# Idle matmuls of the opening read a framework constant instead of a tile that the kernel clears itself

One core of one Trainium2 chip. The metric is the device time of one execution in microseconds, lower is better; the span is the stretch from the first to the last instruction of a profiled execution, some 1.7 us shorter.

## The reference

```python
def reference(q, k, v, n_global, n_local, w_in, w_out, s, b):
    # attention: batch 4, 8 heads, 768 positions, head size 64; a key is kept if it is
    # one of the first 8 positions or one of the 96 positions up to the query
    scores = q @ k.T / sqrt(64) - slope[head] * dist        # others: -1e9
    x = softmax(scores) @ v                                 # heads joined: 3072 x 512
    # feed-forward
    r = maximum(x @ w_in, 0)                                # 512 -> 2048
    return (s * r * r + b) @ w_out                          # 2048 -> 512
```

The outputs are float32; the kernel computes in bf16 with float32 sums.

## The kernel before

The change touches nothing but the first microseconds. The parts that matter, with cuts marked:

```python
    # first loads: k on the queue of SyncE, q on that of ScalarE, in two halves each
    for h2 in range(2):
        for n, eng in enumerate((nc.sync, nc.scalar)):
            f = work.tile([P, H // 2, GB * D], F32, name="first", tag="first", bufs=4)
            eng.dma_start(f[:], pairs_of(srcs[n], 0, h2 * H // 2, H // 2))
            first_f32[h2, n] = f
    nc.scalar.preload_act_table_set("natural_log_exp_and_others")
    # ...
    idle = gpool.tile([P, 4 * P], BF16, name="idle", tag="gsum1", bufs=1)
    nc.vector.memset(idle[:], 0.0)
    for vb in vbuf:
        nc.vector.memset(vb[:, :, :, D:VW], 1.0)
    # ...
    def warm(n, w=2 * P):       # matmuls whose result nobody reads
        ps = ps_h.tile([P, w], F32, name="ps_w", tag="psh")
        for _ in range(n):
            nc.tensor.matmul(ps[:], lhsT=idle[:, 0:P], rhs=idle[:, 0:w], start=True, stop=True)
    # ...
    warm(9, 4 * P)
    cast_first(0, 0, cp)        # first half of k to bf16, VectorE
    cast_first(0, 1, acp)       # first half of q, ScalarE
    # ...
    qk_first(0, 0, cp)          # transposes on TensorE, copied out by VectorE
    qk_first(0, 1, acp)         # the same for q, copied out by ScalarE
    open_bias((0, 1))           # four 128x384 bias matmuls
    cast_first(1, 0, cp)        # second halves
    cast_first(1, 1, acp)
    for part in range(2):       # scores of the first two units
        for i in (0, 1):
            u[i][1](part)
    run(u[0][2])                # exponential of the first unit, ScalarE
    warm(4)
    qk_first(1, 0, cp)          # second halves: transposes and copies
    qk_first(1, 1, acp)
    # ... attention and feed-forward follow, TensorE densely busy
```

The softmax here doesn't subtract the row's maximum and nothing guards it: scores larger than these inputs give would overflow.

## Time and profile before

| | before |
|---|---|
| time, median of the first three executions | 208.71 us (208.68 to 208.73) |
| span of the profiled execution | 207.1 us |
| first idle matmul | 1.20 us into the span |
| first matmul that does work (transposes) | 5.30 us |
| second group of scores, the step at which the opening is done | 9.55 us |

The opening counts because it delays all the rest.

The chain lists what each moment stood on, so an instruction that is not in it delays nothing by its own duration. And TensorE's rate is read from the steps between equal instructions in sequence. The trace itself also keeps a record of the granted clock; its first entry (full) is at 7.15 us, and that is what the steps say too.

### The profile page before, as it was taken

Reading aid. Unit: us, or ns where it says so; the run is one execution under the profiler, and the core shown is the slowest. Engines: PE = TensorE matmul, PEld = TensorE weight load, DVE = VectorE, ACT = ScalarE, POOL = GpSimd, SP = SyncE. Lnnn points to the kernel's source line nnn. Section 1 sums busy time; section 2 is a strip of 40 time slices with the busy share of each in tenths; the row PEclk is TensorE's granted clock in tenths of the full one; section 3 lists DMA queues with packets and bytes.
Section 4 is the critical chain, followed back from the end, with each engine's and each line's share of the span. In section 5 each row is a group of like instructions: output and inputs, shape, how many; then the busy total and the mean of one; then the engine's idle time right before and its main releaser. Section 6 shows DMA issues by size and latency. Waiting matters only on the chain.

```text
span 207.1 us, 5315 instructions
## 1 busy us (share of the span) xinstructions
PE 201.7 (97%) x2183; PEld 160.3 (77%) x2191; DVE 160.7 (78%) x338; ACT 128.4 (62%) x198; POOL 69.7 (34%) x90
## 2 busy tenths in 40 slices
PE   7999999999999999999999999999999999999993
PEld 2678885557876685878888898888888889888883
DVE  7686689977988956799799974699866696737974
ACT  5776669585975648686664595663695764476200
POOL 8985233999455402805502808200000000000000
PEclk9999999999999999999999999999999999999999
DMA  6999999999999999999999999996360300240006
GB/s 162 173 179 200 207 206 177 156 152 136 124 149 134 156 141 224 121 250 209 136 214 181 106 141 179 167 212 69 53 205 3 93 10 3 57 149 0 0 8 197
DMA packets 110836, 28.17 MB, mean 136 GB/s; under 512 B 97852, under 2 KB 109308, under 8 KB 110812
## 3 DMA queue, kind: packets, MB, share of 16 engines
q0 software_dynamic: 76000, 13.11, 86.8%
q1 hardware_dynamic: 33612, 14.13, 37.7%
q10 hardware_dynamic: 1200, 0.59, 1.1%
q8 instruction: 17, 0.28, 0.6%
q14 instruction: 7, 0.06, 0.1%
HBM read 27.26 MB, written 6.29 MB: 162 GB/s over the span
## 4 chain that ended last, share of the span: by engine, by line
PE 95%; DMA 2%; DVE 1%; issue 0%; ACT 0%
PE ps L619 41%; PE ps L819 24%; PE ps L667 13%; PE ps_s L441 6%; PE ps_av L495 5%; DMA first<-in_k_dram 2%; PE ps_t L351 1%; PE ps_s L517 1%; PE ps_t L327 1%; PE ps_x L591 1%; PE ps_s L416 1%; PE ps_s L532 1%; PE ps_av L558 1%; PE ps_t L341 0%; PE ps_last L819 0%
## 5 line engine op out<-in xcount | busy, mean ns | idle before, releaser
L619 PE MATMUL ps<-xT,w_in_bf 128*128 128x256 bf16 x768 | 90.3, 273 | 0.1
L629 ACT ACTIVATE gT<-ps 128x512 bf16<-128x512 f32 x96 | 55.7, 598 | 46.8 <-PE ps L619 46.6
L619 PEld LDWEIGHTS <-w_in_bf 128*128 128x128 bf16 x768 | 73.0, 98 | 9.4 <-DVE xT L594 0.2
L450 ACT ACTIVATE pt<-ps_s 128x1024 bf16<-128x1024 f32 (+1 forms) x44 | 39.3, 946 | 3.0 <-PE ps_s L441 3.0
L667 PE MATMUL ps<-w_out_bf,gT 128*128 128x512 bf16 x120 | 28.7, 380 | 0.5 <-issue 0.2
L457 DVE TENSOR_TENSOR pt<-pt,tmpl 128x1024 bf16<-128x1024 bf16 (+1 forms) x40 | 24.5, 645 | 3.6 <-ACT pt L450 3.5
L819 PEld LDWEIGHTS <-gsum 128*128 128x128 bf16 x256 | 24.1, 98 | 3.8 <-DVE gsum L782 0.5
L108 POOL DMA_DIRECT2D vb<-in_v_dram x24 | 21.4, 907 | 4.3 <-DMA w_out_bf<-in_moe_w_out_dram 3.0
L793 DVE TENSOR_TENSOR gT<-gT 128x1024 bf16<-128x1024 bf16 x20 | 13.7, 687 | 11.7 <-ACT gT L629 11.7
L667 PEld LDWEIGHTS <-gT 128*128 128x128 bf16 x128 | 11.7, 98 | 13.0
L466 DVE TENSOR_TENSOR xn<-ps_av,rc 128x256 bf16<-128x256 f32 x48 | 20.4, 425 | 1.7
L819 PEld LDWEIGHTS <-gT 128*128 128x128 bf16 x200 | 18.6, 98 | 2.3
L465 DVE RECIPROCAL rc<-ps_av 128x4 f32<-128x4 f32 x48 | 8.6, 179 | 12.4 <-PE ps_av L495 10.7
L495 PEld LDWEIGHTS <-pt 128*128 128x128 bf16 x320 | 14.4, 97 | 2.7 <-DVE xn L466 0.7
L632 DVE TENSOR_TENSOR gT<-gT 128x512 bf16<-128x512 bf16 x32 | 12.9, 421 | 3.6 <-ACT gT L629 3.3
L495 PE MATMUL ps_av<-vb,pt 128*128 128x65 bf16 x208 | 15.4, 193 | 0.0
L819 PE MATMUL ps<-w_out_bf,gsum 128*128 128x256 bf16 x128 | 15.3, 273 | 0.0
L819 PE MATMUL ps<-wsub,gsum 128*128 128x256 bf16 x128 | 15.1, 273 | 0.0
L116 POOL DMA_DIRECT2D nat<-in_q_dram x14 | 12.5, 890 | 6.8 <-DMA nat<-in_q_dram 2.8
L116 POOL DMA_DIRECT2D nat<-in_k_dram x14 | 12.4, 884 | 5.8 <-DMA w_in_bf<-in_moe_w_in_dram 2.4
L122 POOL COPY gate<-xT 1x1 bf16<-1x1 bf16 x6 | 1.5, 258 | 37.3 <-DMA xT<-xn 37.3
L819 PE MATMUL ps<-w_out_bf,gT 128*128 128x256 bf16 x120 | 13.9, 273 | 0.0
(112 smaller groups left out, 232.8 us busy)
## 6 DMA issues: line engine op xcount, KB each, us to landing
out_dram<-o_q SPq DMA_DIRECT2D x15, 256.0 KB, 2.5
vb<-in_v_dram POOLq DMA_DIRECT2D x24, 128.0 KB, 7.5
nat<-in_k_dram POOLq DMA_DIRECT2D x22, 128.0 KB, 6.9
nat<-in_q_dram POOLq DMA_DIRECT2D x22, 128.0 KB, 6.9
w_out_bf<-in_moe_w_out_dram POOLq DMA_DIRECT2D x4, 512.0 KB, 16.3
w_in_bf<-in_moe_w_in_dram POOLq DMA_DIRECT2D x4, 256.0 KB, 7.5
w_in_bf<-in_moe_w_in_dram POOLq DMA_DIRECT2D x2, 512.0 KB, 11.5
out_dram<-o_sb SPq DMA_DIRECT2D x4, 256.0 KB, 6.0
```

Source lines behind the costliest of these rows:

```text
L108: nc.gpsimd.dma_start(vbuf[b % 2][:, sb, :, 0:D], rows_of(v, b, sb))
L116: nc.gpsimd.dma_start(t[:, n, i, :, :], rows_of(srcs[n], b, sb))
L450: nc.scalar.activation(pt[:, :, 0:ncol], ps[:, :, 0:ncol], ACT.Exp, scale=QSCALE)
L457: nc.vector.tensor_tensor(pv, pv, m.rearrange("p h a c -> p h (a c)"), ALU.mult)
L466: nc.vector.tensor_tensor(dst, av[:, :, :, 0:D], rc[:].to_broadcast((P, 2, 2, D)), ALU.mult)
L495: nc.tensor.matmul(av[:, i, hi, 0 : D + 1], lhsT=pt[:, hi, c * P : (c + 1) * P], rhs=vv, start=(n == 0), stop=(n == len(terms) - 1),)
L619: nc.tensor.matmul(ps[:, i, :], lhsT=w_in_bf[:, kc, fc * P : (fc + 1) * P], rhs=xT[j][:, kc, :], start=(kc == 0), stop=(kc == KC - 1),)
L629: nc.scalar.activation(gs, ps[:], ACT.Relu)
L632: nc.vector.tensor_tensor(gs, gs, gs, ALU.mult)
L667: nc.tensor.matmul(po[:], lhsT=g_of(j)[:, fc, tb * P : (tb + 1) * P], rhs=w_out_bf[:, fc, :], start=(fc == 0), stop=(fc == FC - 1),)
L793: outs.append(lambda: nc.vector.tensor_tensor(gs, gs, gs, ALU.mult))
L819: nc.tensor.matmul(ps[:, tb, cs], lhsT=stat[:, fc, tb * P : (tb + 1) * P], rhs=mov[:, fc, cs], start=(fc == 0), stop=(fc == NH - 1),)
```

## The change

The idle matmuls run before there is any input, so that TensorE's clock is full when the work comes. (Full clock means here the moment from which equal matmuls follow each other at half the earlier distance: in the trace before, 128x384 matmuls 0.32 us apart at 6.45, and 0.16 us at 8.74; 128x128 transposes 0.107 us apart at 5.49, and 0.056 us at 8.33.) The intent is to start them sooner: they read a constant that the framework writes before it lets the engines go (on GpSimd, at 0.31 us; the first transfers are issued at 0.74), so that no memset on VectorE stands in front of them; the time won is filled by a tenth matmul.

```diff
-    idle = gpool.tile([P, 4 * P], BF16, name="idle", tag="gsum1", bufs=1)
-    nc.vector.memset(idle[:], 0.0)
 # ...
-            nc.tensor.matmul(ps[:], lhsT=idle[:, 0:P], rhs=idle[:, 0:w], start=True, stop=True)
+            nc.tensor.matmul(
+                ps[:],
+                lhsT=nc.const_aps.tensor(1.0, (P, P), BF16),
+                rhs=nc.const_aps.tensor(1.0, (P, w), BF16),
+                start=True,
+                stop=True,
+            )
 # ...
-    warm(9, 4 * P)
+    warm(10, 4 * P)
```

## The prediction

> **What bounds the kernel now.** I started with the first part of the page, the busy shares, to see which engine is the bound over the whole span.
>
> ```profile
> span 207.1 us, 5315 instructions
> PE 201.7 (97%) x2183; PEld 160.3 (77%) x2191; DVE 160.7 (78%) x338; ACT 128.4 (62%) x198; POOL 69.7 (34%) x90
> ```
>
> TensorE's matmuls fill 97% of the span. The chain that ended last says the same: "PE 95%; DMA 2%; DVE 1%". So time is to be had only where TensorE waits or runs slowly, and the change touches only the first 9 us. I therefore asked for the chain of work in that stretch (start, duration, what), because it shows what each microsecond of the opening stands on.
>
> ```profile
> 0.74 3.73 DMA first<-in_k_dram
> 4.46 0.02 issue
> 4.49 0.77 DVE nat L260
> 5.25 0.05 issue
> 5.30 1.04 PE ps_t L327 x8
> 6.34 1.11 PE ps_s L416 x4
> 7.45 0.44 PE ps_s L441 x12
> 7.89 0.54 PE ps_w L161 x4
> 8.44 0.46 PE ps_t L327 x8
> 8.92 0.59 ACT qx L331
> ```
>
> The nine idle matmuls at the start, the ones the change is about, are not in it. The first 4.46 us belong to a load from HBM that is issued at 0.74, then a cast on VectorE; only at 5.30 does TensorE join the path. The four later idle matmuls (0.54 us at 7.89) are in it. The third view is the timeline of the opening (start, duration, engine, line, instruction, count, idle before and its releaser).
>
> ```profile
> 0.86 0.27 DVE L151 MEMSET idle<- 128x256 uint32 x1 [0.86 <-PEq L1235]
> 1.20 4.02 PE L161 MATMUL ps_w<-idle 128*128 128x512 bf16 x9 [1.20 <-DVE idle L151]
> 1.60 0.15 PEld L161 LDWEIGHTS <-idle 128*128 128x128 bf16 x1 [0.28 <-issue]
> 2.02 0.15 PEld L161 LDWEIGHTS <-idle 128*128 128x128 bf16 x1 [0.28 <-issue]
> 4.49 0.76 DVE L260 CAST nat<-first 128x512 bf16<-128x512 f32 x1 [0.36 <-DMA first<-in_k_dram]
> 6.45 0.15 PEld L416 LDWEIGHTS <-open_bf 128*128 128x128 bf16 x1 [0.17 <-issue]
> 6.77 0.15 PEld L416 LDWEIGHTS <-open_bf 128*128 128x128 bf16 x1 [0.17 <-issue]
> ```
>
> The idle matmuls wait until 1.20 for the memset. Two weight loads in sequence lie 0.43 us apart, which is the step from one 128x512 matmul to the next. The 128x384 bias matmuls still step by 0.32 us at 6.45 and 6.77. Later the same form steps by half of that: the pair at 8.74 takes 0.48 us in all and the pair at 10.29 0.49 us, against 1.32 us for the four at 6.13. So TensorE runs at half rate up to about 7.1 us and at full rate from the next matmuls (7.38) on, although the page's row of granted clock shows 9 tenths from the first slice; I trust the steps. The idle matmuls exist to bring that moment forward.
>
> [...]
>
> **The change, part by part.** I compared the instruction order of the two builds on each engine. With line numbers set aside, it differs in three places: one memset fewer at the head of VectorE; no wait in front of TensorE's first weight load; ten instead of nine idle pairs. The later four keep their place. The constant is written by the framework on GpSimd, ahead of the barrier that starts all engines.
>
> Memset: 1 x 0.27 us leaves VectorE. Its followers move up, but the chain on VectorE that ends with a memset at 3.96 to 4.13 then waits for the load that lands at 4.46 (0.36 us of idle before the cast). So this saves nothing on the path: 0.
>
> First start: TensorE no longer waits for the memset. The SyncE and ScalarE queues issue their first transfers at 0.74, the earliest an engine is past the barrier here; TensorE passes it about as late as VectorE or a little earlier (0.86 at most). I take 0.80. The head start is 1.20 - 0.80 = 0.40 us.
>
> Tenth matmul: ten cold ones hold the array for 10 x 0.427 = 4.27 us, from 0.80 to 5.07; nine held it from 1.20 to 1.20 + 9 x 0.427 = 5.04. The transposes can't start before 5.30, when the cast is done. So the tenth fits before them, 0.2 us to spare, and costs 0; it would begin to cost only if the start slipped beyond 5.30 - 4.27 = 1.03.
>
> What is left is the moment of full clock. Every 1.0 us that it comes earlier while TensorE is on the path (5.30 to about 7.4, the transposes and bias matmuls) saves 0.5 us of half-rate work. If the moment follows the first idle matmul, it moves from 7.1 to 6.7: about one bias matmul more runs at 160 instead of 320 ns, and 0.4 x 0.5 = 0.20 us is saved. ScalarE's copy of q (6.37 + 0.59 = 6.96), which the score matmuls also need, allows this: they now start at 7.38 and would start at 7.18. [...]all of the opening is warm: 8 transposes 0.42 us less, 4 bias matmuls 4 x 0.16 = 0.64 us less; but the copies of k and q, behind the casts, hold the scores to about 6.7 (a gain of 0.68), and the second load of q, cast on ScalarE from 6.92 on, together with the first exponential behind it leave about 0.5 us further on.
>
> Is such a gain passed on to the end? No wait for a load shows up on TensorE between 9 and 36 us, and there TensorE is soon dense: 104 matmuls of L619 in 11.42 us from 20.45 on, 0.110 us each. The loads before that have some room: by the trace's landings, the second block of q is in at 11.99 and first used at about 12.6, v at 10.41 for 10.98, the fourth part of w_in at 19.54 for 20.36. So up to about 0.5 us goes through whole.
>
> Sum: 0 (memset) + 0 (tenth matmul) + a clock term between 0 and 0.5, for which I take 0.22 us.
>
> **The rivals.** [...] Third, reading one element with a step of zero could be slow for TensorE[...]. Nine to ten cold matmuls hide that, but the four of 256 columns at 7.83 are on the path, now 0.11 us apart; at half rate they would cost 4 x 0.11 = 0.44 us more: 209.1. [...]
>
> **Range and chances.** I weigh no move of the moment at 35%, a move with the start (0.2 us) at 40%, the jump (0.5 us) at 15%, a loss by the constant's reading at 10%. The mean is 0.40 x 0.20 + 0.15 x 0.5 - 0.10 x 0.44 = 0.11 us, the likeliest single case 0.20; the 0.22 above leans a little to that case and the jump, and gives 208.71 - 0.22 = 208.49. For noise between sessions I add 0.15 us on either side: 208.05 to 208.85. Faster by 2% would need 4.2 us, more than all of the half-rate work on the path; slower by 2% would need a clock that is lost. Both get 1%.
>
> **What would show it.** The first 128x512 idle matmul should start at about 0.8 and not at 1.20, with steps of 0.427 us; the cast at 4.49 and the transposes at 5.30 should stand still within 0.05 us. If they moved, my claim that the memset and the tenth matmul are free is wrong. The steps of the 128x384 bias matmuls tell the clock: all 0.32 us, no move; one more at 0.16, the move; all 0.16, the jump. The score matmuls of L441 should start at about 7.2 and everything after lie earlier by the same amount, up to the end. The four later idle matmuls should stay 0.11 us apart; 0.21 would be the loss by reading a constant. I would be wrong altogether if the transposes waited for the tenth idle matmul, or if the time moved without any of these steps moving.

Passages are cut from this text, with the cuts marked, because they rested on what no run here shows: a rule for the two rates (the rates themselves are measured, 0.32 and 0.16 us from one bias matmul to the next), the reason for the jump, the first, the second and the fourth rival, and part of the third. The forecast's sum: 0 (memset) + 0 (tenth matmul) + 0.22 us (clock) = 0.22 us, and 208.71 - 0.22 = 208.49. The jump is the case in which the clock is full before the transposes start, so that all of the opening runs at full rate ("warm" in the text; "cold" is half rate). Its 0.5 us is an estimate from the steps and durations of the trace before. That such a case can come, the 15% for it and the 35% for no move were my guess. The 0.427 us is the step of the idle matmuls in that trace, (4.583 - 1.596) / 7.

## More of the kernel before

The prediction shows the lines, up to the copy of q that ends at 9.51; the chain goes on with the second group of scores:

```profile
9.55 0.34 PE ps_s L441 x6
```

## The result, and the profile after

The changed kernel took 208.41 us in the median of six executions (208.33 to 209.05), before 208.69 us in six of the same rounds. The ratio is 0.9992, with a 95% interval from 0.9978 to 1.0006: the same. Ratios here are those of the record, which compares the fast runs of the same rounds, so not quite the ratio of the medians. The span of the profiled execution went from 207.1 to 206.6 us.

The timeline of the kernel after, matmuls and first cast of the opening (start, duration, engine, line, instruction, count, idle before and its releaser):

```profile
0.78 4.42 PE L159 MATMUL ps_w<-const-bfloat16-1.0 128*128 128x512 bf16 x10 [0.78 <-PEq L1239]
4.60 0.64 DVE L264 CAST nat<-first 128x512 bf16<-128x512 f32 x1 [0.47 <-DMA first<-in_k_dram]
5.30 0.81 PE L331 MATMUL ps_t<-ident_bf,nat 128*128 128x128 bf16 x8
5.95 0.81 PE L420 MATMUL ps_s<-open_bf 128*128 128x384 bf16 x4
6.79 0.51 PE L445 MATMUL ps_s<-qx,kx 64*128 64x128 bf16 x12
7.23 0.62 PE L159 MATMUL ps_w<-const-bfloat16-1.0 128*128 128x256 bf16 x4
```

The idle matmuls start at 0.78 instead of 1.20, the ten end before the transposes, the cast still waits for its load, the transposes still start at 5.30. The four bias matmuls take 0.81 us in all instead of 1.32: all of them at full rate. The later four idle matmuls take 0.62 us, against 0.61 before (0.113 us from one to the next, against 0.109), so reading one element over and over costs next to nothing. The chain of the kernel after has changed its kind (from 1.25 to 9.31; steps of "issue" of up to 0.04 us are left out here and in the chains below):

```profile
1.25 5.75 DMA first<-in_q_dram
7.02 0.62 ACT nat L264
7.64 0.71 ACT pt L454
8.35 0.58 ACT qx L335
8.97 0.34 PE ps_s L445 x6
```

TensorE is not in it until 8.97. The opening now waits for the second half of q: the load lands at 7.00, ScalarE casts it, computes the first exponential and copies the transposed q out. The second group of scores starts at 8.97 instead of 9.55. The lead of 0.48 us that is left at 11.6 us stays within 0.01 us up to the last group of matmuls. In the chains it starts as follows, first the kernel before, then after:

```profile
203.00 0.91 PE ps_last L819 x16
```

```profile
202.52 0.91 PE ps_last L823 x16
```

So in this pair what is left of the gain is passed on whole. It would be easy to stop here: start 0.42 us sooner, end 0.48 us sooner. But the clock became full at 5.15 us, 2.0 us sooner than before, although the idle matmuls started only 0.42 us sooner. That does not fit a clock that follows its first matmul.

### The profile page after: what moved, and what is told of

It is laid out like the page before. It is cut to its first block, busy times and chain, and to the rows that moved or that the text cites. A ratio compares the mean times of both kernels' runs of the same rounds, so it can differ in the third digit from the quotient of the medians.

```text
span 206.6 us, 5316 instructions
## 1 busy us (share of the span) xinstructions
PE 201.8 (98%) x2184; PEld 160.1 (77%) x2192; DVE 160.4 (78%) x337; ACT 128.3 (62%) x198; POOL 69.7 (34%) x90
## 4 chain that ended last, share of the span: by engine, by line
PE 94%; DMA 3%; ACT 1%; issue 0%; ACTq 0%; DVE 0%
PE ps L623 41%; PE ps L823 24%; PE ps L671 13%; PE ps_s L445 5%; PE ps_av L499 5%; DMA first<-in_q_dram 3%; PE ps_t L355 1%; PE ps_s L521 1%; PE ps_x L595 1%; PE ps_s L536 1%; PE ps_av L562 1%; PE ps_t L345 0%; PE ps_last L823 0%; ACT pt L454 0%; ACT nat L264 0%
## 5 line engine op out<-in xcount | busy, mean ns | idle before, releaser
L623 PE MATMUL ps<-xT,w_in_bf 128*128 128x256 bf16 x768 | 90.3, 273 | 0.1
L623 PEld LDWEIGHTS <-w_in_bf 128*128 128x128 bf16 x768 | 73.0, 98 | 9.4 <-DVE xT L598 0.2
```

The costliest lines, as they stand in the source:

```text
L623: nc.tensor.matmul(ps[:, i, :], lhsT=w_in_bf[:, kc, fc * P : (fc + 1) * P], rhs=xT[j][:, kc, :], start=(kc == 0), stop=(kc == KC - 1),)
```

## The experiments

Two theories stood against each other. **A:** the moment of full clock is a draw: it comes at another moment in each execution, and an earlier start only shifts the range that is drawn from. **B:** the moment follows the first idle matmul by a fixed time, and the change gains 0.5 us in each execution. Twelve runs followed, all with correct results; two of them are the changed kernel unaltered. In each batch of four, the kernels and the kernel before ran on the same chip. The record calls an execution slow when it is over 1.5% above the fastest of the same kernel; unless that is said, the executions are fast ones.

Some expectations are shortened, with the cuts marked: theory A took the limits of the draw, and conditions for it, from a mechanism behind the clock that no run here shows. What a late clock costs in them, half of its delay, is an estimate from the steps (0.32 us against 0.16); the 5.8 us that two of them name is an estimate too, which comes out as 5.65 us below.

### The change again, and its two halves

`after_again` is the changed kernel unaltered.

> The changed kernel unaltered, for more executions. Theory A (the moment of full clock is a draw[...]): the times of single executions spread over 208.3 to 209.1, most at 208.3 to 208.5, mean 0.1 to 0.3 us below before; the profile may show a moment other than 5.15[...]. Theory B (the moment follows the first idle matmul by a fixed time, and the change gains the 0.5 us seen between the two profiles each time): the profile again has it at 5.1, the executions stay within 0.1 us of each other, 0.5 us below before.

Measured: 208.58 us median (208.47 to 208.75), mean 208.61 against 208.63 for before in the same rounds; ratio 0.9999 (0.9987 to 1.0011). The profile shows the full clock at 3.56 us, sooner than ever, and yet a span of 207.0. Its chain:

```profile
1.25 6.10 DMA first<-in_q_dram
7.37 0.62 ACT nat L264
7.99 0.71 ACT pt L454
8.70 0.58 ACT qx L335
9.33 0.34 PE ps_s L445 x6
```

The durations of the work are those of the first profile after; the load landed 0.35 us later, and the scores started 0.36 us later. (The first load of k was late by as much, 4.93 against 4.58, so the transposes started at 5.43 here.) B is out: the moment after the first idle matmul was 4.37 us in one profile and 2.78 in the other. And something else than the clock is a bound: this execution, with the earliest clock of all, took 208.75 us, so the spread of single times isn't the clock's alone.

`const_nine` is the constant alone:

```diff
-    warm(10, 4 * P)
+    warm(9, 4 * P)
```

> The constant alone: nine idle matmuls from 0.78, over by 4.65, then TensorE idle for 0.6 us until the transposes at 5.30. Theory A: mean within 0.15 us of the changed kernel[...]. Theory B: as the changed kernel, 208.4.

Measured: 208.57 us median, mean 208.59, ratio 1.0000 (0.9987 to 1.0013); full clock at 4.38 us. No difference from the changed kernel (208.61) can be told, as A allowed.

`memset_ten` is the tenth matmul alone, in the kernel before:

```diff
-    warm(9, 4 * P)
+    warm(10, 4 * P)
```

> The tenth matmul alone, with the memset kept: the first at 1.20, ten at half rate hold the array to 5.47, so the transposes wait about 0.17 us beyond 5.30 in executions that are still at half rate. Theory A: mean 0 to 0.15 us above before, 208.7 to 208.85. Theory B (the start sets all): as before, 208.7.

Measured: 208.57 us median, mean 208.65, ratio 1.0001 (0.9988 to 1.0014). In its chain TensorE stands from 1.19 us on, and the tenth matmul delays the transposes:

```profile
1.19 4.45 PE ps_w L161 x10
5.64 0.85 PE ps_t L327 x8
6.49 0.92 PE ps_s L416 x4
```

The transposes started at 5.44 (the chain puts the idle matmuls' ends at 5.64), 0.14 us late. So the tenth is free only together with the earlier start. In the mean nothing of it can be seen.

### A later start

`late_start` goes the opposite way: the kernel before, with the memset behind further VectorE work and five idle matmuls.

```diff
-    idle = gpool.tile(...); nc.vector.memset(idle[:], 0.0)     # first on VectorE
 # ... behind the mask's compare and scale:
+    idle = gpool.tile(...); nc.vector.memset(idle[:], 0.0)
     nc.vector.tensor_copy(base_bf[:, 1:3, :], ...)
 # ...
-    warm(9, 4 * P)
+    warm(5, 4 * P)
```

> The opposite of the change, larger: the memset is put behind two more VectorE instructions, so that five idle matmuls start at about 3.0 and end at 5.1. Theory A: [...]0.3 to 0.7 us slower than before in the mean, with few executions under 208.7. Theory B: moment 1.8 us later than the 7.15 of before, at about 8.9, time 0.5 us up in each execution. A third theory (idle matmuls matter little, the difference is memset against constant): within 0.1 us of before.

Measured: 209.00 us median (208.56 to 209.75), mean 209.12, 0.49 us above before; ratio 1.0024 (1.0007 to 1.0041). The first idle matmul came at 2.90. The four later ones, at 8.3, show the clock change: the first two lie 0.185 us apart, the next 0.109. So it became full at about 8.46 (this trace has no record of the clock), and the second group of scores started at 10.10. The mean fits both A and B; the spread of single executions, 1.2 us, is what A expects. The third theory (idle matmuls matter little) is out. The edit changes two things at once, the start and the number of idle matmuls; in both kernels the last of them starts at 4.58 us.

### No idle matmuls at the start

`no_idle`, and once more as `no_idle_again`: the changed kernel without `warm(10, 4 * P)`.

> The changed kernel without the ten idle matmuls of the start. Theory A, as it stands now ([...]the moment of full clock is a draw[...], and costs half of what it lies beyond about 5.8 us): the first matmul is the transposes at 5.30[...], and the kernel is 0.8 to 2 us slower than the changed one. If the idle matmuls don't matter: within 0.2 us.

> No idle matmuls at the start, once more. Normal executions should again be 1 to 2 us slower than the changed kernel. Open is the single execution of 345.76 us, at a granted clock of 0.56 from 10.2 us to the end: if having no idle matmuls brings it about, one of these six should show it again; if it was an event of the chip, none will.

Measured: the second time 210.16 us median (209.29 to 210.47), ratio 1.0071 (1.0047 to 1.0095); the first time, the five fast executions, 1.0069 (1.0047 to 1.0091). That is 1.4 to 1.5 us above before of the same rounds. The second profile has the full clock at 9.93, and the opening in its chain runs at half rate:

```profile
5.29 1.04 PE ps_t L331 x8
6.33 1.28 PE ps_s L420 x4
7.61 0.76 PE ps_s L445 x12
8.36 0.97 PE ps_w L159 x4
9.33 0.81 PE ps_t L331 x8
```

One execution of the first batch took 345.76 us. It was the profiled one, and it isn't used in any mean or ratio. Its record has a granted clock of 0.56 from 10.2 us to the end, where all others that have a record go to 1.00. The steps bear it out: the 128x256 matmuls of L623 are mostly 0.20 us apart, against 0.11 in the trace after (in the median one lasts 365 ns, against 273). The busy times and the clock by stretches (stretch, then span share in us, PE, PEld, DVE, ACT, POOL busy with counts, granted clock, DMA share, GB/s):

```profile
0.00:10.00 10.00, 4.71 (x37) 3.25 (x38) 5.69 (x17) 5.22 (x11) 9.21 (x16) 1.00 1.38 167
10.00:20.00 10.00, 9.91 (x107) 6.59 (x106) 6.59 (x20) 6.08 (x8) 7.98 (x12) 0.56 1.69 187
```

The later stretches, up to 344 us, show 0.56 too. (The 1.00 of the first stretch is not to be trusted: the transposes at 9.12 still step by 0.107 us, half rate.) None of the six executions of the second time, on another chip, did it again. What brought it about stays open; a single event doesn't tell whether the missing idle matmuls had a part in it.

### The memset on its own

`memset_kept`, twice: the changed kernel, with the tile cleared on VectorE all the same, read by nobody.

```diff
+    idle = gpool.tile([P, 4 * P], BF16, name="idle", tag="gsum1", bufs=1)
+    nc.vector.memset(idle[:], 0.0)
     for vb in vbuf:
```

> The changed kernel, reading the constant, but VectorE still writes the tile that nobody reads. If the memset itself costs nothing on the path (as predicted): the mean of its executions within 0.12 us of the changed kernel's 208.56, the first idle matmul at 0.78, the cast of the first load still waiting for that load. If the memset's 0.27 us were on the path: 0.25 us slower than the changed kernel.

> The memset kept once more, since its first six executions had a mean of 208.79, higher than expected, with one at 209.24. If that was the draw: mean within 0.12 us of the changed kernel in these rounds, and the trace again shows the first cast waiting for its load. If the memset costs something by a way that the trace did not show: again 0.2 us above it.

Measured: first 208.78 us median, mean 208.79, which is 0.23 us above the mean that I had expected to meet within 0.12: a miss. It is 0.06 us above before in its rounds. The second time 208.53 us median, mean 208.53 against 208.56 for the changed kernel on the same chip in the same rounds (ratios to before 1.0001 and 1.0002). Both profiles have the first idle matmul at 0.78. In the second one's timeline, VectorE:

```profile
0.86 0.27 DVE L151 MEMSET idle<- 128x256 uint32 x1 [0.86 <-PEq L1241]
4.42 0.82 DVE L266 CAST nat<-first 128x512 bf16<-128x512 f32 x1 [0.29 <-DMA first<-in_k_dram]
```

VectorE has gone through all its work before the cast and waits another 0.29 us for the load (0.56 us in the first profile). So the memset is not on the path. What made the first batch slower is not shown. In its profile the clock was full late, at 6.26, and the cast of q's first half began late, at 5.13; but that execution, at 208.61 us, is one of the faster of the six.

### The load of q as a floor

`q_late` was meant to move the second load of q behind the activation table load, and `q_later`, after that failed, behind an activation.

```diff
 # q_late, in the loop of the first loads
+            if h2 and n:
+                nc.scalar.preload_act_table_set("natural_log_exp_and_others")
             eng.dma_start(f[:], pairs_of(srcs[n], 0, h2 * H // 2, H // 2))
 # q_later
-    diagonal(range(0, 6))
+    diagonal(range(0, 1))
+    nc.scalar.dma_start(first_f32[1, 1][:], pairs_of(srcs[1], 0, H // 2, H // 2))
+    diagonal(range(1, 6))
```

> The changed kernel with the second load of q issued behind the activation table load, some 1.3 us later. Theory A has a floor: in executions where the clock is early the opening ends with this load, its cast, one exponential and the copy of q, 1.97 us after the landing at about 7.0. Then the time rises by as much as the landing moves, 0.3 to 1.0 us. If TensorE alone set the opening, the landing could move to about 7.5 without a change: within 0.15 us.

> The second load of q issued by ScalarE behind its first activation (about 3.4 us into the span); the first attempt had failed to move the load, since the queue did not wait for the table load. With a floor (load of q, cast, exponential, copy, 1.97 us in all after the landing): the landing moves from 6.8 to 7.4 up to 7.5 to 9, and the kernel is slower by about that, 0.4 to 1.5 us. Without one: within 0.15 us of the changed kernel.

Measured: 208.49 us median (208.32 to 208.58), ratio 0.9987 (0.9972 to 1.0001), and 208.40 us median (208.33 to 208.84), ratio 0.9998 (0.9979 to 1.0017). Both edits failed in what they were to do. The timeline of `q_late`, then of `q_later`, shows ScalarE's queue issuing the second load at 1.28 and 1.48, beside the table load (which moved from 1.88 to 1.25 and 1.26) and ahead of the first activation (2.54 and 2.55):

```profile
1.28 0.57 ACTq L131 DMA_DIRECT2D first<-in_q_dram  x1
```

```profile
1.48 0.37 ACTq L240 DMA_DIRECT2D first<-in_q_dram  x1
```

The loads landed at 6.82 and 6.87, as early as in others. So no run moved the load on purpose. What speaks for the floor is its own variation, with the moment of full clock at 5.2 us or before each time:

| profile | full clock | load of q landed | second scores | between |
|---|---|---|---|---|
| const_nine | 4.38 | 6.78 | 8.78 | 2.00 |
| memset_kept_again | 4.97 | 6.80 | 8.80 | 2.00 |
| q_later | 4.83 | 6.87 | 8.85 | 1.98 |
| after | 5.15 | 7.00 | 8.97 | 1.97 |
| after_again | 3.56 | 7.35 | 9.33 | 1.98 |

Over 0.57 us of landing times, the scores follow within 0.03 us, and the order is that of the landings, not of the clock. The floor is therefore read from five traces, not shown by an edit.

`no_four` takes away the four later idle matmuls, `warm(4)`, from the changed kernel.

> The changed kernel without the four later idle matmuls (0.44 us of TensorE). With the floor (load of q, cast, exponential, copy): nothing gained where the clock is early, up to 0.4 us gained where it is late, in the mean 0 to 0.15 us faster. Without a floor (TensorE alone on the path): 0.44 us faster each time. If the four are needed to reach or keep the clock: slower by 0.2 us or more.

Measured: 208.43 us median (208.28 to 208.72), ratio 0.9987 (0.9972 to 1.0002). TensorE saves 0.44 us there, and the time falls by 0.27 us in the mean against before in its rounds; against all 17 executions of the changed kernel, on several chips, it is 0.09 us lower. Nowhere near 0.44 below the changed kernel. In its chain the floor stands again:

```profile
6.80 0.62 ACT nat L264
7.42 0.72 ACT pt L454
8.18 0.49 PE ps_s L420 x2
8.66 0.33 PE ps_s L445 x6
```

The copy of q (0.58 us) left the chain; the scores came 1.88 us after the landing at 6.78, 0.1 us less than in the table above. The full clock was neither lost nor late: the four bias matmuls from 5.78 on took 0.81 us, as at full rate in the profile after, and the two at 8.18 took 0.49 us. This is the fastest version by its median in these rounds, but the interval includes 1, so I don't call it better than either kernel.

### The size of the effect

`after_third` is the changed kernel a third time.

> The changed kernel once more, for the size of the effect. Theory A with[...] a cost of half of what the moment lies beyond 5.8 us: mean 0.05 to 0.15 us below the mean of before in the same rounds, single executions between 208.3 and 209.1. Theory B (fixed gain of 0.5 us each time): 0.5 us below.

Measured: 208.56 us median (208.37 to 208.73), ratio 1.0002 (0.9983 to 1.0021). The mean is 0.06 us above before in these rounds, not 0.05 to 0.15 below: a miss of the size, while a fixed gain of 0.5 us is out for good. On this chip nine of the eleven executions of before fell between 208.29 and 208.43, and one at 209.63, so the draws of one batch may not be independent. Its profile has the full clock at 6.77, and its chain is that of the kernel before again, with TensorE on the path:

```profile
5.30 1.03 PE ps_t L331 x8
6.33 0.93 PE ps_s L420 x4
7.26 0.44 PE ps_s L445 x12
...
9.37 0.34 PE ps_s L445 x6
```

Put together, 17 executions of the changed kernel have a mean of 208.55 us, 39 of the kernel before 208.63 us: 0.075 us, with a standard error of 0.067. But eleven of these 39 come from a batch in which the changed kernel did not run. In the three batches that had both, it gained 0.165, 0.017 and -0.057 us: 0.04 us in the mean, with a standard error of 0.07. A gain of zero is not excluded, one of 0.5 us is.

## Why the prediction was right or wrong

The prediction said 208.49 us, between 208.05 and 208.85, the same within 2%. The first measurement was 208.41, and all 17 executions have a mean of 208.55. By the prediction's own signs, the first profile after was its jump (all bias matmuls 0.16 us apart, the first scores at 6.79), to which it gave 15%, and not the move that it took as likeliest. By its steps:

- **The memset costs nothing on the path.** Right. The traces before and after have the cast waiting for its load, and so have both of memset_kept; keeping the memset changed nothing that a second batch bore out.
- **The first idle matmul starts at 0.80.** Right: 0.78.
- **The tenth is free.** Right with the earlier start: the steps of 0.427 us bring ten of them from 0.78 to 5.05, and the transposes start at 5.30 in the profiles before and after. Without the earlier start it delayed the transposes to 5.44.
- **Each microsecond of an earlier full clock saves half.** Right in kind, and close in size. Where TensorE is on the path, the second scores started at 9.37, 9.55, 10.10 and 10.80 for a full clock at 6.77 (after_third), 7.15 (before), 8.46 (late_start) and 9.93 (no_idle_again). That is (10.80 - 9.37) / (9.93 - 6.77) = 0.45 us for each us. Three more profiles with TensorE on the path lie 0.06 to 0.12 us above this line: q_late (8.96 for 5.73), memset_kept (9.26 for 6.26) and memset_ten (9.52 for 6.91), the last two with transposes that were partly late.
- **The load of q and ScalarE hold the gain to about 0.5 us.** Right in kind; at the end of the opening (12 us) the profiles with an early clock are 0.14 to 0.67 us ahead of before, by when the load lands. Crossing the line of 0.45 with the floor (scores at about 8.87, for a load landed at 6.89 as in before) gives 9.37 - 0.45 x (6.77 - m) = 8.87, m = 5.65: a clock that is full before about 5.65 us gains nothing more. This is an estimate; with a load that lands at 7.35, as in after_again, the same sum gives 6.7.
- **How the moment of full clock responds to the start** was the weak step. I gave most weight to a move with the start. Against a moment that wanders from execution to execution (a rival) I held that three executions lay within 0.05 us. That argument was wrong: with more executions, before spreads from 208.29 to 209.63 (how much of this is the clock and how much the loads is not separated). In thirteen profiles (no_idle's first left out, before and after in), the full clock came 2.78 to 5.98 us after the first matmul, in no order with the start: a range of 3.2 us. What sets the moment within this range is not shown.
- **The gain passes to the end.** Right for after: 0.48 us at 11.6 us and at the end; after_again and after_third kept theirs too. In `const_nine`, though, 0.18 of 0.67 us was lost again at about 41 us, in `memset_kept_again` 0.22 of 0.64 between 41 and 115 us, and in `q_later` 0.57 of 0.62 between 57 and 95 us, where its chain has the transposed loads of q and x in place of TensorE. So an early clock is not always worth its gain at the end: `q_later`, full at 4.83, took 208.84 us.

The size follows as an estimate from these numbers. Assume that the full clock is drawn evenly from the range that the thirteen profiles span, 2.78 to 5.98 us after the first matmul, and costs 0.45 us for each us beyond 5.65. Before (from 1.20): drawn from 3.98 to 7.18, mean cost 0.45 x 1.53² / 2 / 3.20 = 0.16 us. After (from 0.78): 3.56 to 6.76, 0.45 x 1.11² / 2 / 3.20 = 0.09 us. The difference is 0.08 us, where 0.04 to 0.075 was measured, with zero not excluded. The same sum gives 0.57 us for late_start (0.49 measured) and 1.6 us for no idle matmuls (1.4 to 1.5 measured); slope, bound and range come from some of the same traces, so this is a check of consistency. The predicted 0.22 us was thus too large by a factor of about three by this estimate, and lies about two standard errors or more above what was measured. It was also double the 0.11 us that the prediction's own chances gave. The term that was mis-sized is the clock term: the full 0.40 us of head start times one half was booked for the whole, where only the draws beyond 5.65 us pay at all.

The right number came partly by luck: five of the six executions behind the first median were among the fastest of the 17 (208.33 to 208.45). Only one of them was traced, with a full clock at 5.15 us, so that the others had early clocks too is likely but not shown.

## What to carry to other kernels

An effect whose moment differs between executions (here the full clock, by 3.2 us) is a distribution: compare means of many executions, and look at the profile only to learn the mechanism, since one pair of profiles showed 0.48 us where the mean moves less than 0.1. Idle matmuls before the first input are worth having (1.4 to 1.5 us here), but once they have started early enough, another 0.4 us of them bought nothing that could be measured, because in the profiles with an early clock the next load is the bound. To see whether a change worked, test the dose: first matmuls at 0.78, 1.20, 2.90 and 5.29 us told more than repeats of the change.
